# One decode layer on Trainium2: K and V loaded by 512 keys of all heads, weights turned on VectorE, one running sum

## The chip, the cores and the metric

The kernel runs on one core of one Trainium2 chip. The time is that of one execution on the device, in microseconds (us), the median of several runs.

## The reference

One token of two sequences goes through a transformer layer: layer norm, attention over a window of a cache, a residual, layer norm, a gated feed-forward part, a residual. All tensors are bf16.

```python
# x: [2, 1, 640]; k_cache, v_cache: [2, 32, 8192, 192]; wq: [640, 6144]; wo: [6144, 640]
# w_gate, w_up: [640, 1536]; w_down: [1536, 640]
W = min(4096, max(256, 8192 // 4))                     # 2048 keys
q = (layernorm(x) @ wq).reshape(B, 1, 32, 192)          # 32 query heads, 32 K/V heads
k, v = k_cache[:, :, -W:, :], v_cache[:, :, -W:, :]
p = softmax(einsum("bhqd,bhkd->bhqk", q, k) * 192 ** -0.5)
o = einsum("bhqk,bhkd->bhqd", p, v).reshape(B, 1, 6144)
h = x + o @ wo
h2 = h + (gelu(layernorm(h) @ w_gate) * (layernorm(h) @ w_up)) @ w_down
```

With one query per head every byte of K and V is used once: 2 sequences x 32 heads x 2048 keys x 192 x 2 bytes is 50.3 MB for K and the same for V. With the weights the kernel reads 122.3 MB.

## The kernel before

**Groups.** The work is cut into 16 groups `g`. A group is four heads of one sequence with all 2048 keys: partition 4i+h holds 64 consecutive keys (`TPG`) of one head, a run of 24 KB. So K of a group is one transfer of 3 MB, V another (`kv_src`, `load_k`, `load_v`). Four groups make a `J`: the same eight heads of both sequences, which is 1536 rows of wo.

**The ring.** All large transfers go to one SBUF tensor `ring` of 144 KB per partition, cut into six slots of 24 KB: four places for K, two for V, and weights that lie over them at times. `load` puts a transfer in a list in program order; `pump` issues the head of the list once every earlier tenant of its bytes has been told `done`. All of them are issued by SyncE (SP) in that order, so a transfer that waits for its bytes holds back those behind it. The issue stands at L369 of the profile.

**One group on the engines.** `transposes(g, half)` (L579) turns K in pairs of bf16 values seen as float32: three times per half eight TensorE (PE) transposes into one of two PSUM buffers `tpp`, and an eviction to `ktr`, by VectorE (DVE, L593) for the first and third, by ScalarE (ACT, L589) for the second. `scores(g)` (L640) multiplies them with the queries `rq`, masked per head by GpSimd (POOL); DVE adds a mask and takes the maximum (`sm`, `mx`, L649). `softmax(g)` spreads the maximum over the partitions by a small matmul (L656), and ACT takes the exponential (L660) with its row sums `zr`. `e_columns(g)` turns the weights by four matmuls on `sel64` and a masked product on DVE into `ering`. `pv(g)` (L685) multiplies 32 such stationaries with V and accumulates four groups in one PSUM bank `ops`.

**The end of a J.** `z_rows`, `o_rows` and `o_columns` divide by the sum and turn the result into columns `ot` (L699, L709, the DVE product `orow`, L717, L721); `oproj(J)` (L735) multiplies them with its part of wo and adds into `hrow`.

**Order.** Each engine runs its instructions in program order. `_Prog` finds the waits. PE and DVE run the groups in a loop over J, in which e_columns and pv of a group come between the halves of the next group's transposes and behind them:

```python
scores(4 * J)
softmax(4 * J)
for g in range(4 * J + 1, 4 * J + 4):
    transposes(g, 0)
    e_columns(g - 1)
    transposes(g, 1)
    pv(g - 1)
    scores(g)
    softmax(g)
```

K of group 0 is loaded first, then wq, then K of group 1. Behind the loop come `oproj(3)` (L735, L745), the second layer norm (L752 to L813) and the feed-forward part (L824 to L880).

Of the kernel before, what the change touches and what calls it, by code (L numbers as in the profile page):

```python
# [5 lines left out]
BF16 = mybir.dt.bfloat16  # L6
# [6 lines left out]
B = 2  # L13
# [16 lines left out]
WO_BIAS = 32  # L30
RARE = ("oc", "q", "y0")
# [200 lines left out]
SLOT = 24576  # L232
RING = 6 * SLOT
TPG = 64
# [7 lines left out]
WU_AT = K_AT[2]  # L242
WD_AT = (K_AT[2] + 15360, 15360, 19200, 19200 + 2560)


def bass_sequential_preLN__sliding_block_cached__geglu_ffn__decode_kernel(
# [12 lines left out]
    with ExitStack() as ctx:  # L259
# [14 lines left out]
        selw = sb("selw", [128, 2, 128], F32)  # L274
        zsel = sb("zsel", [128, 128], F32)
        mska = sb("mska", [128, 128], F32)
        oh4 = sb("oh4", [128, 4], F32)
        oh16 = sb("oh16", [128, 16], F32)
        mask = sb("mask", [128, 6, 4], F32)
        mask16 = sb("mask16", [128, 16], F32)  # L280
        maskhd = sb("maskhd", [128, 8], F32)
        sel64 = sb("sel64", [128, 64], BF16)
        selq = sb("selq", [128, 32], BF16)
        selb = sb("selb", [128, 2], BF16)
        eps_t = sb("eps_t", [128, 1], F32)
# [27 lines left out]
        rq = sb("rq", [128, 4, 6, 16], BF16)  # L313
        qs = sb("qs", [128, 384], BF16)
        mx = sb("mx", [128, 1], F32)
        mrhs = sb("mrhs", [128, 16], BF16)
        sm = sb("sm", [128, 512], F32)
        gate = sb("gate", [128, 1], F32)
        nm = sb("nm", [128, 1], F32)
        zr = sb("zr", [128, 4], F32)  # L320
        z4 = sb("z4", [128, 4], F32)
        zs = sb("zs", [128, 1], F32)
        rinv = sb("rinv", [128, 1], F32)
        wm = sb("wm", [128, 8], F32)
        eexp = sb("eexp", [128, 512], BF16)
        ering = sb("ering", [128, 4, 32, 32], BF16)
        osb = sb("osb", [128, 384], F32)
        orow = sb("orow", [128, 8, DH], BF16)
        cti = orow[:, :, :].rearrange("p h d -> p (h d)").bitcast(I32)[:, 0:512].rearrange("p (k x) -> p k x", k=4)
        ot = sb("ot", [128, 12, B], BF16)  # L330
# [4 lines left out]
        urow = osb  # L335
# [12 lines left out]
        P.dma_count["wo"] = WO_BIAS  # L348
# [26 lines left out]
        def kv_src(cache, g):  # L375
            h0 = 8 * (g // 4) + 4 * (g % 4 // 2)
            return cache[g % 2, h0:h0 + 4, SKT - WIN:, :].rearrange("h (i t) d -> i h (t d)", t=TPG)

        def load_k(g):
            load(("k", g), K_AT[g % 4], SLOT, kv_src(A_k_cache, g), lambda v: v, f"k{g % 4}")  # L380

        def load_v(g):
            load(("v", g), V_AT[g % 2], SLOT, kv_src(A_v_cache, g), lambda v: v, f"v{g % 4}")
# [5 lines left out]
        def load_wo(J):  # L389
            src = A_wo[1536 * J:1536 * (J + 1), :].rearrange("(p kk) n -> p kk n", kk=12)  # L390
            for i, (k0, k1) in enumerate(wo_parts(J)):
                load(("wo", J, i), WO_AT[J] + 2 * k0 * D, 2 * (k1 - k0) * D, src[:, k0:k1, :],
                     lambda v: v.rearrange("p (kk n) -> p kk n", n=D), "wo" if J < 3 else f"wo{J}{i}")

        def wo_parts(J):
            return ((0, 12),)
# [5 lines left out]
        def load_ffn():  # L402
            load(("wg", 1), K_AT[1], 2 * (NC5 - 1) * F, B_w_gate.rearrange("(p c) f -> p c f", c=NC5)[:, 1:NC5, :],
# [34 lines left out]
        load_k(0)  # L438
        load_wq()
        load_k(1)  # L440
        for g in range(NG):
            if g > 0 and g + 1 < NG:
                load_k(g + 1)
            load_v(g)
            if g % 4 == 3 and g > 3:
                load_wo(g // 4 - 1)
        load_wo(3)
# [3 lines left out]
        BITS = (1, 2, 3, 6, 12, 16, 28, 31, 32, 64, 96)  # L451
# [5 lines left out]
        pool(lambda e: e.memset(ering[:, :, :, :].rearrange("p a b c -> p (a b c)").bitcast(I32), 0), W=[("er", k) for k in range(4)])  # L457
# [12 lines left out]
        dve(tt(pti[:, :], pi[:, :].to_broadcast([128, 11]), bits[:, :], ALU.bitwise_and),  # L470
            R=["pi"] + [("bits", k) for k in range(11)], W=["pti"])
# [40 lines left out]
        for k, pat in enumerate(([[0, 32], [1, 4]], [[0, 16], [2, 4], [0, 2]], [[0, 4], [4, 8], [0, 4]], [[32, 4], [0, 32]])):  # L512
            pool(lambda e, k=k, pat=pat: e.iota(cti[:, k, :], pattern=pat, base=0, channel_multiplier=0), W=[("cti", k)])
        pool(lambda e: e.tensor_copy(cf[:, 1:5, :], cti[:, :, :]), R=[("cti", k) for k in range(4)], W=["cfm"])


        pool(ts(pg[:, 1:2], rb(31), 16.0, ALU.is_lt), R=["pf"], W=["v16"])
        pool(ts(pg[:, 2:3], rb(31), 4.0, ALU.is_lt), R=["pf"], W=["v4"])
        pool(ts(pg[:, 4:5], rb(16), 8.0, ALU.mult, rb(3), ALU.add), R=["pf"], W=["c16"])
        pool(ts(pg[:, 5:6], rb(96), 0.125, ALU.mult, pg[:, 4:5], ALU.add), R=["pf", "c16"], W=["c16b"])  # L520
        pool(ts(pg[:, 6:7], rb(96), 0.5, ALU.mult, rb(1), ALU.add), R=["pf"], W=["c64"])
        pool(ts(pg[:, 7:8], rb(12), 0.5, ALU.mult, pg[:, 6:7], ALU.add), R=["pf", "c64"], W=["c64b"])
        pool(ts(pg[:, 6:7], rb(2), 4.0, ALU.mult, pg[:, 7:8], ALU.add), R=["pf", "c64b"], W=["c64"])
        pool(ts(pg[:, 7:8], rb(16), 64.0, ALU.mult, pg[:, 6:7], ALU.add), R=["pf", "c64"], W=["c64b"])
# [3 lines left out]
        pool(ts(pg[:, 10:11], rb(64), 1.0 / 16.0, ALU.mult, rb(31), ALU.add), R=["pf"], W=["chd"])  # L528
        pool(ts(pg[:, 11:12], rb(3), 2.0, ALU.mult), R=["pf"], W=["p3"])
# [8 lines left out]
        pool(ts(pm[:, :], cf[:, 3, :], rb(28), ALU.is_equal), R=["cfm", "pf"], W=["pm"])  # L538
        pool(ts(oh16[:, :], cf[:, 0, 0:16], pg[:, 5:6], ALU.is_equal), R=["cf0", "c16b"], W=["oh16"])
        pool(ts(sel64[:, :], cf[:, 0, 0:64], pg[:, 7:8], ALU.is_equal), R=["cf0", "c64b"], W=["sel64"])  # L540
        pool(ts(mask16[:, :], cf[:, 2, 0:16], pg[:, 11:12], ALU.is_equal), R=["cfm", "p3"], W=["mask16"])
        pool(ts(mska[:, :], cf[:, 1, :], 4.0, ALU.mult, rb(12), ALU.is_equal), R=["cfm", "pf"], W=["mska"])
        pool(ts(zsel[:, :], mska[:, :], pg[:, 1:2], ALU.mult), R=["mska", "v16"], W=["zsel"])
        pool(ts(mska[:, :], mska[:, :], -1.0, ALU.add, BIG, ALU.mult), R=["mska", "zsel"], W=["mska"])

        def consts_late():
            pool(ts(oh4[:, :], cf[:, 0, 0:4], pg[:, 8:9], ALU.is_equal), R=["cf0", "cq"], W=["oh4"])
            pool(ts(cf[:, 1, :], cf[:, 1, :], 2.0, ALU.mult), R=["cfm", "mska"], W=["cf1"])
            pool(ts(cf[:, 4, :], cf[:, 4, :], 0.25, ALU.mult), R=["cfm"], W=["cf4"])
            pool(tt(cf[:, 1, :], cf[:, 1, :], cf[:, 4, :], ALU.add), R=["cf1", "cf4"], W=["cf1"])  # L550
            pool(ts(cf[:, 3, :], cf[:, 3, :], 1000.0, ALU.mult), R=["cfm", "pm"], W=["cf3"])
# [374 lines left out]
```

## Time and profile before

| | |
|---|---|
| median of three runs | 292.94 us (292.73 to 293.17) |
| profiled execution: time | 292.85 us |
| profiled execution: span of the core | 291.5 us |
| mean granted TensorE clock | 0.874 |
| PE, DVE, ACT, POOL busy | 199.5, 123.8, 76.9, 25.7 us |
| moved by DMA | 122.42 MB at a mean of 420 GB/s |

The page has the busy time of each engine, the span in 40 equal slices (a digit is a share in tenths, GB/s what the DMA engines moved), the chain of waits that ended last, the costliest groups of instructions, and the DMA issues with their size and time to landing. A row of the timeline is: start and length in us, engine, line of the kernel, operation, what is written from what, shapes, count, and in brackets how long the engine had been idle and what ended that. A row of the groups has the busy time of all and the mean length of one in ns.

### The profile page before, as it was taken

How to read it: one execution, taken by the hardware profiler on the slowest of the kernel's cores; microseconds unless marked ns; L12 is line 12 of the kernel's file. 1: busy time of each engine (PE TensorE's matmuls, PEld its weight loads, DVE VectorE, ACT ScalarE, POOL GpSimd, SP SyncE). 2: the span in 40 equal slices, each digit the busy share in tenths (PEclk: the TensorE clock that was granted, in tenths of full speed). 3: DMA queues.
4: the chain of work that ended last, by engine and by line, in shares of the span. 5: the costliest groups of instructions: out<-in, count | busy, mean ns of one | idle time of the engine just before them, and what ended most of it. 6: DMA issues, size and time to landing. Idle time of an engine off the chain costs nothing.

```text
span 291.5 us, 5193 instructions
## 1 busy us (share of the span) xinstructions
PE 199.5 (68%) x2141; PEld 145.3 (50%) x2141; DVE 123.8 (42%) x232; ACT 76.9 (26%) x72; POOL 25.7 (9%) x85
## 2 busy tenths in 40 slices
PE   0670768756866587877776848684957848686885
PEld 0550445636555285654654727362835547563443
DVE  5250035632535444645165525362563525352422
ACT  1050123332232033532320513251313315151001
POOL 8891020000000000000000000000000000000000
PEclk9996699997979779999599998999799969797555
DMA  8999999999999999999999999999999999999994
GB/s 324 432 465 396 430 432 425 427 430 428 428 432 432 432 432 432 432 432 432 416 440 432 432 432 432 429 425 432 424 440 432 428 432 432 432 432 411 426 414 159
DMA packets 6505, 122.42 MB, mean 420 GB/s; under 512 B 734, under 2 KB 864, under 8 KB 1504
## 3 DMA queue, kind: packets, MB, share of 16 engines
q1 hardware_dynamic: 6348, 121.90, 97.7%
q10 hardware_dynamic: 148, 0.40, 0.5%
q8 instruction: 6, 0.10, 0.1%
q14 instruction: 3, 0.02, 0.0%
HBM read 122.29 MB, written 0.00 MB: 419 GB/s over the span
## 4 chain that ended last, share of the span: by engine, by line
DMA 58%; PE 23%; DVE 7%; issue 6%; ACT 4%; SPq 1%; DVEq 0%
DMA ring<-in_A_k_cache_dram 44%; PE tpp L579 12%; DMA ring<-in_A_wq_dram 10%; DMA ring<-in_A_wo_dram 5%; DVE ktr L593 4%; ACT ktr L589 3%; PE ops L685 3%; PE tpp L603 2%; DVE orow L434 1%; PE m L709 1%; PE m L735 1%; SPq L369 1%; DVE ering L434 1%; PE sps L824 1%; PE m L873 1%
## 5 line engine op out<-in xcount | busy, mean ns | idle before, releaser
L579 PE MATMUL tpp<-identf,ring 128*128 128x128 f32 x768 | 113.5, 308 | 38.4 <-DMA ring<-in_A_k_cache_dram 21.0
L579 PEld LDWEIGHTS tpp<-identf,ring 128*128 128x128 f32 x768 | 99.0, 159 | 48.8 <-DMA ring<-in_A_k_cache_dram 22.0
L593 DVE COPY ktr<-tpp 128x2048 bf16<-128x2048 bf16 x64 | 78.4, 1225 | 86.8 <-PE tpp L579 86.4
L589 ACT ACTIVATE ktr<-tpp 128x2048 bf16<-128x2048 bf16 x32 | 60.1, 1877 | 83.6 <-PE tpp L579 83.6
L660 ACT ACTIVATE eexp<-sm,nm 128x512 bf16<-128x512 f32 x16 | 11.5, 722 | 84.3 <-DVE nm L658 84.3
L640 PE MATMUL sps<-ktr,rq 128*16 128x512 bf16 x384 | 25.8, 403 | 1.2 <-POOL rq L434 1.2
L685 PE MATMUL ops<-ring,ering 128*32 128x384 bf16 x512 | 25.0, 340 | 0.0
L649 DVE CUSTOM_DVE_ANT_1 sm<-sps,mska 128x512 f32<-128x512 f32 x16 | 11.0, 686 | 27.9 <-issue 27.9
L434 POOL TENSOR_TENSOR rq<-qs,mask 128x96 bf16<-128x96 bf16 x16 | 5.5, 354 | 170.7 <-PE sps L640 156.7
L685 PEld LDWEIGHTS ops<-ring,ering 128*32 128x32 bf16 x512 | 12.5, 99 | 8.1 <-issue 2.5
L640 PEld LDWEIGHTS sps<-ktr,rq 128*16 128x16 bf16 x384 | 8.7, 89 | 13.9 <-issue 6.6
L656 PE MATMUL m<-mrhs,pm 128*128 128x16 bf16 x16 | 2.9, 184 | 17.2 <-DVE mrhs L430 17.2
L656 PEld LDWEIGHTS m<-mrhs,pm 128*128 128x128 bf16 x16 | 1.5, 96 | 26.0 <-DVE mrhs L430 26.0
L603 PE MATMUL tpp<-ring,xnT 128*32 128x384 bf16 x80 | 5.3, 444 | 9.4 <-DMA ring<-in_A_wq_dram 9.4
L434 DVE TENSOR_TENSOR orow<-m,wm 128x1536 bf16<-128x1536 f32 x4 | 7.0, 1758 | 4.1 <-PE m L709 4.1
L603 PEld LDWEIGHTS tpp<-ring,xnT 128*32 128x32 bf16 x80 | 3.0, 127 | 11.6 <-issue 9.6
L434 DVE TENSOR_TENSOR ering<-m,mask 128x256 bf16<-128x256 f32 x16 | 6.6, 415 | 1.3 <-PE m L669 1.3
L626 DVE CAST qs<-ops 128x384 bf16<-128x384 f32 x1 | 0.6, 557 | 15.0 <-PE ops L621 15.0
L717 PE MATMUL m<-selb,orow 128*128 128x2 bf16 x48 | 3.5, 200 | 4.2 <-DVE orow L434 4.2
L717 PEld LDWEIGHTS m<-selb,orow 128*128 128x128 bf16 x48 | 3.2, 156 | 5.8 <-DVE orow L434 5.8
L709 PE MATMUL m<-osb,selw 128*128 128x192 f32 x16 | 4.4, 405 | 1.9 <-DVE osb L695 1.9
L735 PE MATMUL m<-ring,ot 128*2 128x320 bf16 x96 | 5.5, 381 | 0.0
(124 smaller groups left out, 91.5 us busy)
## 6 DMA issues: line engine op xcount, KB each, us to landing
ring<-in_A_k_cache_dram SPq DMA_DIRECT2D x16, 3072.0 KB, 32.3
ring<-in_A_v_cache_dram SPq DMA_DIRECT2D x16, 3072.0 KB, 26.7
ring<-in_A_wq_dram SPq DMA_DIRECT2D x1, 7680.0 KB, 28.2
ring<-in_A_wo_dram SPq DMA_DIRECT2D x4, 1920.0 KB, 16.3
ring<-in_B_w_gate_dram SPq DMA_DIRECT2D x1, 1536.0 KB, 17.7
ring<-in_B_w_up_dram SPq DMA_DIRECT2D x1, 1536.0 KB, 20.9
ring<-in_B_w_down_dram SPq DMA_DIRECT2D x1, 960.0 KB, 23.3
ring<-in_B_w_down_dram SPq DMA_DIRECT2D x1, 480.0 KB, 24.0
```

Source lines behind the costliest of these rows:

```text
L434: return lambda e: e.tensor_tensor(out=out, in0=a, in1=b, op=op)
L579: ins = e.transpose(tpp[bi][:, 512 * j + 128 * u:512 * j + 128 * (u + 1)], kv[:, off:off + 128], identf[:, :])
L589: act(lambda e, dst=dst, bv=bv: e.activation(out=dst, in_=bv, func=ACT.Copy), W=[("kt", half, k)], X=both)
L593: dve(lambda e, dst=dst, bv=bv: e.tensor_copy(dst, bv.rearrange("p (a x) -> p a x", a=2)), W=[("kt", half, k)], X=both, cls=0)
L603: ins = e.matmul(tps[0][32 * r:32 * (r + 1), 0:384], lhsT=xnT[:, c, 32 * J:32 * (J + 1)], rhs=wq[:, c, 1536 * J + 384 * r:1536 * J + 384 * ...
L640: ins = e.matmul(sps[32 * ch:32 * ch + 16, :], lhsT=rq[:, g % 4, k, :], rhs=ktr[:, k // 2, 1024 * ch + k % 2:1024 * (ch + 1):2], start=(k ...
L649: dve(lambda e: e.tensor_tensor_reduce(out=sm[:, :].rearrange("p (u x) -> p u x", u=4), in0=sps[:, :].rearrange("p (u x) -> p u x", u=4), ...
L660: act(lambda e: e.activation(out=eexp[:, :], in_=sm[:, :], func=ACT.Exp, bias=nm[:, 0:1], scale=1.0, accum_out=zr[:, g % 4:g % 4 + 1]), R= ...
L685: ins = e.matmul(ops_[32 * r:32 * (r + 1), 0:384], lhsT=ering[:, g % 4, t, :], rhs=vv[:, 384 * t:384 * (t + 1)], start=(g % 4 == 0 and t < 4),
L709: pe(lambda e, tp=tp: e.matmul(bank, lhsT=selw[:, tp, :], rhs=osb[:, DH * tp:DH * (tp + 1)], start=(tp == 0), stop=(tp == 1), skip_group_c ...
L717: ins = e.matmul(m2[:, 2 * kk:2 * kk + 2], lhsT=orow[:, :, kk:DH:12], rhs=selb[:, :], start=True, stop=True)
L735: ins = e.matmul(m1[32 * r:32 * r + 2, 192:512], lhsT=ot[:, kk, :], rhs=wo[:, kk - k0, 320 * h:320 * (h + 1)], start=(kk == 1 or J < 3 and ...
```

## The change

- **Loads.** A load is now 512 consecutive keys of all 32 heads of one sequence: partition 4h+r holds 128 keys, a run of 48 KB, 6 MB in all. The ring has three slots of 48 KB: two for K, one for V. A load serves a pair of groups, `2i` and `2i+1`, each with 64 of the 128 keys of every partition. wq is loaded first, before K. All four parts of wo are loaded behind the last V, before the feed-forward weights.
- **Weights.** `e_columns` and its matmuls go; `e_blocks(g)` turns the exponentials by four DVE transposes in blocks of 32x32, one for each quarter of the partitions, into `eblk`.
- **pv.** Each group has 64 matmuls of 192 columns in a bank of its own (`ops` or `m1`), copied to `osb`; pv of both groups of a pair stands behind the second group's softmax and e_blocks.
- **Running sum.** After four groups `weights` and `combine` scale the four results and the sum so far to a common maximum and add them in `osum`. After 8 groups, one sequence, `heads_done(b)` divides and turns the result into columns.
- **wo.** All four `oproj` stand behind the loop, with one accumulation in PSUM.
- **Queries.** `q_rows` stands ahead of the loop, with 64 of its matmuls cut to 192 columns, 112 in all; `rq` is masked in four parts at the start of a sequence.

The core of the diff, with the constants and masks that go with it left out:

```diff
-SLOT = 24576
-RING = 6 * SLOT
-TPG = 64
+SLOT = 49152
+RING = 3 * SLOT
+TPG = 128
+NQ = 4
...
-K_AT = (0, SLOT, 3 * SLOT, 5 * SLOT)
-V_AT = (2 * SLOT, 4 * SLOT)
-WQ_AT = 3 * SLOT + SLOT // 2
-WO_AT = (K_AT[3], K_AT[3], K_AT[3], 0)
+K_AT = (0, SLOT)
+V_AT = 2 * SLOT
+WQ_AT = SLOT
+WO_AT = (0, 15360, 30720, SLOT)
...
-            return cache[g % 2, h0:h0 + 4, SKT - WIN:, :].rearrange("h (i t) d -> i h (t d)", t=TPG)
+        def kv_src(cache, i):
+            t0 = SKT - WIN + NQ * TPG * (i % NQ)
+            return cache[i // NQ, :, t0:t0 + NQ * TPG, :].rearrange("h (r t) d -> h r (t d)", t=TPG)
+
+        def load_k(i):
+            load(("k", i), K_AT[i % 2], SLOT, kv_src(A_k_cache, i), lambda v: v, f"k{i % 2}")
+
+        def load_v(i):
+            load(("v", i), V_AT, SLOT, kv_src(A_v_cache, i), lambda v: v, f"v{i % 2}")
...
-        load_k(0)
         load_wq()
-        load_k(1)
-        for g in range(NG):
...
+        for i in range(2 * NQ):
+            load_k(i)
+            load_v(i)
+        for J in range(4):
+            load_wo(J)
         load_ffn()
...
+        def weights():
+            dve(lambda e: e.tensor_reduce(out=nmin[:, :], in_=nms[:, :], axis=AX.X, op=ALU.min), ...
+            act(lambda e: e.activation(out=wz[:, 0:5], in_=nms[:, :], func=ACT.Exp, bias=nmin[:, 0:1], scale=-1.0), ...
+
+        def e_blocks(g):
+            for hg in range(4):
+                dve(lambda e, hg=hg: e.transpose(eblk[32 * hg:32 * (hg + 1), g % 2, :, hg, :],
+                                                 eexp[32 * hg:32 * (hg + 1), :].rearrange("p (a x) -> p a x", x=32)),
+                    R=["eexp"], W=[("eb", g % 2, hg)], cls=0)
+
+        def pv(g):
+            vv, vtoks = where["v", g // 2]
+            bank, x = ((ops_, "o"), (m1, "m1"))[g % 2]
 
             def fn(e):
...
+                for a in range(16):
+                    for r in range(4):
+                        t = 64 * (g % 2) + 4 * a + r
+                        ins = e.matmul(bank[32 * r:32 * (r + 1), 0:DH],
+                                       lhsT=eblk[:, g % 2, a, :, :].rearrange("p s x -> p (s x)")[:, r:128:4],
+                                       rhs=vv[:, DH * t:DH * (t + 1)], start=(a == 0), stop=(a == 15),
+                                       tile_position=(0, 32 * r), skip_group_check=True)
                 return ins
...
+            if g % 2 == 1:
+                done(("v", g // 2))
+            dve(lambda e: e.tensor_copy(osb[:, g % 4, :], bank[:, 0:DH]), W=[("osb", g % 4)], X=[x], cls=0)
+
+        def combine():
+            dve(lambda e: e.tensor_tensor_reduce(out=z5[:, :], in0=wz[:, 0:5], in1=zr[:, :], ...
+            dve(lambda e: e.tensor_copy(zr[:, 4:5], wz[:, 5:6]), ...
+            dve(lambda e: e.tensor_copy(nms[:, 4:5], nmin[:, :]), ...
+            pe(lambda e: e.matmul(m2[:, 264:270], lhsT=rowsel[:, :], rhs=wz[:, :], start=True, stop=True), ...
+            dve(lambda e: e.tensor_scalar(out=wp[:, :], in0=m2[:, 264:270], scalar1=0.25, scalar2=None, op0=ALU.mult), ...
+            dve(ts(osum[:, :], osum[:, :], wp[:, 4:5], ALU.mult), R=["wp", "osum"], W=["osum"], cls=0)
+            for k in range(4):
+                dve(lambda e, k=k: e.scalar_tensor_tensor(out=osum[:, :], in0=osb[:, k, :], scalar=wp[:, k:k + 1], in1=osum[:, :], ...
+
+        def heads_done(b):
+            dve(lambda e: e.reciprocal(rinv[:, :], wp[:, 5:6]), R=["wp"], W=["rinv"])
+            dve(ts(onrm[:, :], osum[:, :], rinv[:, 0:1], ALU.mult, 0.25, ALU.mult), ...
...
+            for y in range(2):
+                def fn(e, y=y):
+                    for j in range(2):
+                        J = 2 * y + j
+                        ins = e.matmul(sps[:, DH * j:DH * (j + 1)], lhsT=colsel[:, 128 * J:128 * (J + 1)], rhs=onrm[:, :],
+                                       start=True, stop=True, skip_group_check=True)
+                    return ins
+
+                pe(fn, R=["colsel", "onrm"], X=["s"])
+                dve(tt(sm[:, 0:384]..., sps[:, 0:384]..., mask16..., ALU.mult), R=["mask16"], W=["sm"], X=["s"])
+                dve(lambda e: e.tensor_reduce(out=ot32[:, :], in_=sm[:, 0:384]..., axis=AX.X, op=ALU.add), ...
+                dve(lambda e, y=y: e.tensor_copy(ot[:, 2 * y:2 * y + 2, :, b], ot32[:, :]...), R=["ot32"], W=["ot"])
...
+        q_rows()
+        q_stationary()
         looped.append(True)
-        for J in range(5):
...
+        for J in range(4):
+            P.loop_seg("a", J)
+            for g in range(4 * J, 4 * J + 4):
+                transposes(g, 0)
+                if g % 2 == 1:
+                    e_blocks(g - 1)
+                transposes(g, 1)
+                scores(g)
+                softmax(g)
+                if g % 4 == 3:
+                    weights()
+                if g % 2 == 1:
+                    e_blocks(g)
+                    pv(g - 1)
+                    pv(g)
+            combine()
+            if J == 1:
                 P.loop_seg("op", J)
-                oproj(J - 2)
...
+                heads_done(0)
         P.loop_seg()
-        oproj(3)
+        heads_done(1)
+        for J in range(4):
+            oproj(J)
```

More of the change, by code (lines that the diff above doesn't have):

```diff
@@ L29 @@
 BIAS = 16
-WO_BIAS = 32
-RARE = ("oc", "q", "y0")
+RARE = ()
 class _Op:
@@ L389, in load_wo @@
         def load_wo(J):
[L390 to L396, printed above, removed]
+            load(("wo", J), WO_AT[J], 24 * D, A_wo[1536 * J:1536 * (J + 1), :].rearrange("(p kk) n -> p kk n", kk=12),
+                 lambda v: v.rearrange("p (kk n) -> p kk n", n=D), f"wo{J}")
         def load_wg0():
@@ L583, in transposes @@
                 pe(fn, R=ktoks + ["identf"], X=both)
-                if half == 1 and k == 2:
-                    done(("k", g))
+                if g % 2 == 1 and half == 1 and k == 2:
+                    done(("k", g // 2))
                 bv = tpp[bi][:, :].bitcast(BF16)
@@ L706, in o_rows @@
-        def o_rows(J):
-            bank = m2[:, 276:276 + DH]
-            for tp in range(2):
-                pe(lambda e, tp=tp: e.matmul(bank, lhsT=selw[:, tp, :], rhs=osb[:, DH * tp:DH * (tp + 1)], start=(tp == 0),
-                                             stop=(tp == 1), skip_group_check=True), R=[("osb", tp), ("selw", tp)], X=["m2o"])
-            dve(tt(orow[:, :, :], bank.unsqueeze(1).to_broadcast([128, 8, DH]),
-                   wm[:, :].unsqueeze(2).to_broadcast([128, 8, DH]), ALU.mult), R=["wm"], W=["orow"], X=["m2o"])
@@ new lines, in softmax @@
+            dve(lambda e: e.tensor_reduce(out=nms[:, n:n + 1], in_=m2[:, 256:260], axis=AX.X, op=ALU.max, negate=True),
+                W=[("nm", n)], X=["m2"], cls=0)
+            act(lambda e: e.activation(out=eexp[:, :], in_=sm[:, :], func=ACT.Exp, bias=nms[:, n:n + 1], scale=1.0,
+                                       accum_out=zr[:, n:n + 1]), R=[("nm", n), "sm", "gate"], W=["eexp", ("zr", n)])
+        def weights():
+            dve(lambda e: e.tensor_reduce(out=nmin[:, :], in_=nms[:, :], axis=AX.X, op=ALU.min), R=[("nm", k) for k in range(5)],
+                W=["nmin"], cls=0)
+            act(lambda e: e.activation(out=wz[:, 0:5], in_=nms[:, :], func=ACT.Exp, bias=nmin[:, 0:1], scale=-1.0),
+                R=["nmin"] + [("nm", k) for k in range(5)], W=["wz"])
```

312 lines of the change are left out of this document (116 added, 196 removed).

## The prediction

> **What bounds it now.** I read the page from the top: span, slices, the chain that ended last; then the DMA issues, and the queue's own waits (engine, line, releaser: us in total, times, longest).
>
> ```profile
> span 291.5 us, 5193 instructions
> ...
> DMA  8999999999999999999999999999999999999994
> GB/s 324 432 465 396 430 432 425 427 430 428 428 432 432 432 432 432 432 432 432 416 440 432 432 432 432 429 425 432 424 440 432 428 432 432 432 432 411 426 414 159
> ...
> DMA 58%; PE 23%; DVE 7%; issue 6%; ACT 4%; SPq 1%; DVEq 0%
> ...
> ring<-in_A_k_cache_dram SPq DMA_DIRECT2D x16, 3072.0 KB, 32.3
> ...
> ring<-in_A_wq_dram SPq DMA_DIRECT2D x1, 7680.0 KB, 28.2
> ring<-in_A_wo_dram SPq DMA_DIRECT2D x4, 1920.0 KB, 16.3
> ...
> SPq L369 <- PE ops L685: 123.0, 11, 17.1
> ```
>
> The transfers bind: every slice but the ends moves about 432 GB/s. A K or V load (3072 KB, 3.146 MB) takes 7.28 us at that rate; K and V of one group 14.56 us. The queue waits long for V buffers (123 us), but with earlier loads still moving, so the rate never falls. The profiled execution took 292.85 us, span plus 1.35; the median of the runs, 292.94, agrees. What counts is how much shorter than 14.56 us a group's arithmetic is. The timeline of group 1 (start, length, engine, line):
>
> ```profile
> 40.49 1.96 PE L579 MATMUL tpp<-identf,ring 128*128 128x128 f32 x16
> ...
> 42.49 1.88 ACT L589 ACTIVATE ktr<-tpp 128x2048 bf16<-128x2048 bf16 x1 [0.84 <-PE tpp L579]
> ...
> 44.03 1.22 DVE L593 COPY ktr<-tpp 128x2048 bf16<-128x2048 bf16 x1 [1.19 <-PE tpp L579]
> ...
> 45.17 0.41 DVE L434 TENSOR_TENSOR ering<-m,mask 128x256 bf16<-128x256 f32 x1
> 45.55 1.22 DVE L593 COPY ktr<-tpp 128x2048 bf16<-128x2048 bf16 x1
> ...
> 46.83 1.09 PE L579 MATMUL tpp<-identf,ring 128*128 128x128 f32 x8 [0.43 <-DVE ktr L593]
> ...
> 47.85 1.48 PE L685 MATMUL ops<-ring,ering 128*32 128x384 bf16 x32
> 47.96 1.22 DVE L593 COPY ktr<-tpp 128x2048 bf16<-128x2048 bf16 x1 [1.19 <-PE tpp L579]
> ...
> 49.31 1.55 PE L640 MATMUL sps<-ktr,rq 128*16 128x512 bf16 x24
> ...
> 50.93 0.69 DVE L649 CUSTOM_DVE_ANT_1 sm<-sps,mska 128x512 f32<-128x512 f32 x1 [1.74 <-issue]
> ...
> 51.95 0.18 PE L656 MATMUL m<-mrhs,pm 128*128 128x16 bf16 x1 [1.08 <-DVE mrhs L430]
> 52.17 0.17 DVE L658 TENSOR_REDUCE nm<-m 128x1 f32<-128x16 f32 x1 [0.28 <-PE m L656]
> 52.38 0.72 ACT L660 ACTIVATE eexp<-sm,nm 128x512 bf16<-128x512 f32 x1 [4.00 <-DVE nm L658]
> 52.48 1.97 PE L579 MATMUL tpp<-identf,ring 128*128 128x128 f32 x16 [0.35 <-DMA ring<-in_A_k_cache_dram]
> 53.01 0.19 ACT L660 ACTIVATION_READ_ACCUMULATOR eexp<-sm,nm 128x1 f32 x1
> ```
>
> From the first transpose at 40.49 to the end of the maximum's matmul at 52.13 is 11.64 us; only then does PE wait for K. Its exponential (52.38) runs under the next group's transposes, and pv (47.85) fits exactly under the last eviction (47.96 to 49.18), ahead of scores. So 2.9 us of each 14.56 are slack, and nothing of a group's softmax is exposed.
>
> **The pair.** A load is now 6.29 MB, 14.56 us, for two groups; K has two slots, V only one. Per pair the two loads are 29.1 us, with the same bytes as before. Four edits act on the PE order.
>
> (1) In the even group pv is gone from under the last eviction, but scores waits for that eviction anyway: 11.64 us stay. Scores and maximum keep their shapes, the weights' load 32 columns instead of 16; taken at nothing, since it overlaps the streams (a tenth of scores, 0.15 us, if not).
>
> (2) Four DVE transposes of 32 partitions by 512 bf16 replace the four matmuls on sel64 and the 0.41 us product. No row has such a transpose. Rows for its price:
>
> ```profile
> L593 DVE COPY ktr<-tpp 128x2048 bf16<-128x2048 bf16 x64 | 78.4, 1225 | 86.8 <-PE tpp L579 86.4
> ...
> 215.10 0.62 DVE L695 COPY osb<-ops 128x192 f32<-128x192 f32 x2 [0.80 <-PE ops L685]
> ...
> 287.62 1.78 PE L873 MATMUL m<-ring,uT 128*17 128x160 bf16 x48 [0.31 <-DVE uT L434]
> ```
>
> The plain copy moves an element in 0.6 ns (1225 for 2048), so 0.3 us for 512; the product above takes 1.62 ns, so 0.83 us; sm, 512 one at a time, takes 0.69. I take sm's row as nearest, less a little overlap between neighbours (two osb copies need 0.62): 0.62 each, E = 2.5 us a group; bounds 1.2 and 3.3. The Trainium skill (VectorE: DVE Perf Modes, section The three transpose paths) gives 311 ns for a 128x128 bf16 transpose on VectorE; my estimate from that page by plain scaling to 512 elements a row is 1.24 us each, 5 us a group, and the sum below would then be 40 us longer; no row here shows it.
>
> In the odd group E stands on DVE between the evictions of the two halves, where the product pushed the 45.55 eviction by 0.3: the odd group ends its maximum after 11.64 - 0.3 + 2.5 = 13.84 us.
>
> (3) pv of both groups follows in PE order, ahead of the next transposes. pv(g-1) hides under the softmax, pv(g) does not: from the maximum's matmul to exp's release 1.2 us (52.13 to 53.2 and a wake-up), then E again, then pv(g): 0.1 + V. V is 64 matmuls of 192 columns. By columns it is the 1.48 of today's 32 of 384; by count it would be 46 ns each, 2.9 us. The L873 row issues 48 of 160 columns at 37 ns in the slow end of the kernel; I take 30 ns, V = 1.9. So 1.2 + 2.5 + 0.1 + 1.9 = 5.7 us stand bare, with PE idle for about 1.8 of them.
>
> Pair: C = 11.64 + 13.84 + 5.7 = **31.2 us**, against 29.1 of loads.
>
> (4) The one V buffer. V of the next pair is issued when pv(g) of this one is done, some 2 us before data flows (below), and K after next queues behind it on SP. So K after next lands 31.1 us after this pair's end: the queue runs dry whenever C is over 27.1, and at C = 31.2 period and pair length are equal. What is queued behind the new waits: on PE everything, on DVE the next evictions, on SP the next K.
>
> **The boundaries.** Every second pair ends in weights and combine. Rows for these, for the tail and for the start:
>
> ```profile
> 1.44 0.57 SPq L369 DMA_DIRECT2D ring<-in_A_wq_dram  x1
> ...
> 29.82 5.29 PE L603 MATMUL tpp<-ring,xnT 128*32 128x384 bf16 x80 [9.40 <-DMA ring<-in_A_wq_dram]
> ...
> 215.52 0.92 PE L709 MATMUL m<-osb,selw 128*128 128x192 f32 x4 [0.46 <-DVE osb L695]
> ...
> 218.23 0.48 DVE L434 TENSOR_TENSOR hrow<-m,hrow 98x320 f32<-98x320 f32 x1
> ...
> 266.84 0.59 PE L699 MATMUL m<-zr,zsel 128*128 128x4 f32 x2 [0.52 <-DVE ering L434]
> ...
> 275.91 1.77 PE L735 MATMUL m<-ring,ot 128*2 128x320 bf16 x24
> ...
> 277.73 0.49 DVE L745 CUSTOM_DVE_ANT_0 hrow<-m,hrow 98x320 f32<-98x320 f32 x1 [2.46 <-PE m L735]
> ...
> 282.72 0.62 DVE L430 TENSOR_SCALAR sm<-sps,rstd 98x384 f32<-98x384 f32 x1 [1.86 <-PE sps L824]
> ...
> 289.80 0.69 SPq L880 DMA_DIRECT2D out_dram<-yrow  x1
> ```
>
> Combine: osb copy 0.35 and the sum of weights 0.3, the float32 matmul 0.6 as L699, wp 0.2, then osum in five DVE passes over 192 elements, 0.33 each by hrow's 0.48 for 320. PE goes on after 1.4 us, but its first eviction waits behind osum: 2.2 us per boundary, 3.3 to the end of osum; weights' reduce adds 0.2 on the four odd pairs. The old o_rows and o_columns (orow and its matmuls) go, but they stood in DMA slack. heads_done: 0.6 for two small DVE operations, and for each half a float32 matmul pair (0.92) and on DVE 0.6 + 0.6 + 0.2 (sm's size); the second half's matmul overlaps the first's reduce: 4.8 us; in the middle, once, 4.3 of it delay the next eviction.
>
> Start: K0 came first and then wq, landing at 29.8 with 11.01 MB (25.5 us of transfer): 4.2 us are latency and slow first slice. wq and a double K0 are 14.16 MB: K0 lands at 37.0. q_rows, split into 112 matmuls, hides under K0; if it did not, V0 alone would come later. Of these I take 2 us as the time from an issue to its first bytes; were it 4, the last pv would come no later: each K then lands 33.1 us after a pair's end, and the next pair with the boundary before or behind it (2.2) takes 33.4.
>
> Loop: 37.0 + 8 x 31.2 + 3 x 2.2 + 4.3 + 0.8 = 298.3 for the last pv. Tail: osum 3.3, heads_done 4.8, then all of wo: 4 x 1.77 + 0.4 = 7.5 (three of these four stood under loads); from there 277.7 to the span's end at 291.5, 13.8: together 29.4. wo, gate, up, down (13.4 MB, 31 us) follow V7 (issued at about 267 + 2, landed at 283) and end at 314: under the tail. Span 327.7, time **329.0 us**, 36 slower, 12%.
>
> **The rivals.**
>
> *The loads keep binding* (the other side). Place: the wait of V(i+1). It decides at C = 27.1 us; below that, the loads run back to back as now. E of 0.3 (0.07 us a transpose) and V = 1.5 give C = 26.4; with boundaries of 1 us instead of 2.2 the last K lands at 37.0 + 14 x 14.56 = 240.8, the last pv is done at 267.2 and the transfers at 286.4. Today they end about 286.9 (2.7 us of the last slice at 432), 4.6 before the span; so the span is 291, the time 292.3, no change, if the tail runs at full clock (half of 7.1 for wo and 3 us less behind it: 22.9). With the 29.4 it is 298. For it: the slack of 2.9 us a group. Against: two groups' own chains are 23.3 us before any transpose of weights, and E would have to lie under the plain copy's. 4%, half of it not slower.
>
> *All heads at once slows the reads.* 32 heads lie 8192 x 192 x 2 bytes = 3 MiB apart, and the 16 engines now start at such distances; today a load takes four heads and its engines mostly read neighbouring runs. The rows show full rate with four heads, and no wider load. It decides from 403 GB/s down (two loads longer than 31.2 us). At the 324 GB/s of the first slice, a load is 19.4 us, K0 lands at 42, and the loop is 38.8 a pair: 374 + 1.4 = 375 us; at 396, the lowest full slice, 331. The Trainium skill (DMA: Bandwidth & Descriptors, section Latency and other measured facts, on row pitch) speaks against this layout: copies with rows 2 MiB apart ran at 164 GB/s where 512 KiB apart gave 207. By that ratio, an estimate from the page, a load would take 18.4 us. No run here shows it; 3 MiB is no power of two. 9%.
>
> *The clock drops at each pair's end.* A granted clock seen when PE waits:
>
> ```profile
> core 0: us, PE busy (x) PEld busy (x) DVE busy (x) ACT busy (x) POOL busy (x), PEclk, DMA share, GB/s
> 266.00:275.00 9.00, 7.77 (x78) 4.34 (x78) 3.77 (x9) 0.00 (x0) 0.00 (x0) 0.50 1.00 424
> ...
> 67.42 4.51 PE L579 MATMUL tpp<-identf,ring 128*128 128x128 f32 x24 [3.32 <-DMA ring<-in_A_k_cache_dram]
> ```
>
> After 3.3 us idle, 24 transposes take 4.5 us where 3.4 are usual, and two waits of 1.1 us within 2.4 us put the tail at 0.50. The new wait has 1.1 + 1.8 us idle with pv between. If pv(g) and the first transposes run at half clock, a pair is 2 us longer: 345 us. 15%.
>
> **How the numbers follow.** The pair-bound case has 72%; its bounds are E = 1.2 with V = 1.5 (C = 28.25, where the queue's 31.1 shares in the period: 308) and E = 3.3 with V = 2.9 (C = 33.85: 350). The range starts a little under, at 305, for a tail at full clock, and ends at 352, with the clock rival inside and the slow reads left out: 8 in 10. About 0.2% (0.6 us) is what a measurement of this kernel can tell from no change. Faster 0.02, same 0.02, slower 0.96.
>
> **What would show it.** Right: DVE transposes of about 0.6 us, PE idle 1.5 to 2 us just before every second pv, SP's V wait ended by that pv with the DMA engines empty (slices of 7 to 8 tenths in the middle), K landed before PE asks, and some 29 us from the last pv to the end, the last 13 without a transfer. Wrong: slices of 9 throughout at a lower GB/s (reads), slices of 9 at 432 (loads still bind), a clock of 0.5 at pair ends, or transposes far from 0.6 us.

## The result and the profile after

The changed kernel takes **355.68 us**, the median of six runs (348.51 to 359.93), against 292.84 us (292.55 to 293.32): ratio 1.191, 95% interval 1.188 to 1.194. Two of the six runs took 348.5 and 349.3 us at a granted clock of 0.88 to 0.89 and four took 354 to 360 us at 0.79 to 0.84, and the ratios in this document go by runs of the first kind. The forecast was 329.0 us in a range of 305 to 352: by the ratio the time is 349 us, inside it near its upper end, while the median of all six lies 4 us above it. The profiled execution took 349.29 us, 20.3 more than the forecast's sum.

The page of the changed kernel, from the top: span, clock by slices, the DMA engines by slices, the chain that ended last; then groups (line, engine, operation, tiles, count | busy us, mean ns | idle before, what ended it), DMA issues, and the queue's own wait.

```profile
span 347.7 us, 6049 instructions
...
PEclk9999978569959998999697998997899888988579
DMA  9999999629995999499959980799699949999950
GB/s 351 453 418 424 381 435 401 263 92 452 449 424 212 424 407 441 164 430 401 452 226 407 452 363 0 311 413 452 271 362 452 447 187 362 410 426 434 415 218 2
...
PE 29%; DVE 28%; issue 25%; DMA 11%; ACT 5%; DVEq 1%; SPq 0%; ACTq 0%
...
L555 PE MATMUL tpp<-identf,ring 128*128 128x128 f32 x768 | 105.4, 292 | 45.4 <-DVE ktr L569 34.9
...
L651 DVE STREAM_TRANSPOSE eblk<-eexp 32x512 bf16<-32x512 bf16 x64 | 44.9, 701 | 7.8 <-ACT eexp L640 6.3
L620 PE MATMUL sps<-ktr,rq 128*32 128x512 bf16 x384 | 35.4, 517 | 22.3 <-DVE ktr L569 22.3
...
ring<-in_A_k_cache_dram SPq DMA_DIRECT2D x8, 6144.0 KB, 31.6
ring<-in_A_v_cache_dram SPq DMA_DIRECT2D x8, 6144.0 KB, 17.5
...
SPq L370 <- PE m L663: 252.5, 8, 40.5
```

DMA was 58% of the chain and is now 11%; the DMA row has a hole in the middle once a pair, as the forecast asked for, and the queue's eight waits all end with pv on the m bank, the second of a pair. Between the holes the engines move up to 453 GB/s, so the long runs are not read more slowly. The mean granted clock, 0.882, is no lower than before (0.874); but a fall now lengthens the chain, where before there was slack. One pair, from its first transpose to the issue of the next V (start, length, engine, line; in brackets the engine's idle time and what ended it):

```profile
143.28 1.96 PE L555 MATMUL tpp<-identf,ring 128*128 128x128 f32 x16
...
152.11 1.54 PE L620 MATMUL sps<-ktr,rq 128*32 128x512 bf16 x24 [1.39 <-DVE ktr L569]
...
154.85 0.18 PE L636 MATMUL m<-mrhs,pm 128*128 128x4 bf16 x1 [1.20 <-DVE mrhs L426]
154.89 1.95 PE L555 MATMUL tpp<-identf,ring 128*128 128x128 f32 x16
...
157.27 1.09 PE L555 MATMUL tpp<-identf,ring 128*128 128x128 f32 x8 [0.44 <-DVE ktr L569]
...
159.54 2.89 DVE L651 STREAM_TRANSPOSE eblk<-eexp 32x512 bf16<-32x512 bf16 x4
...
163.75 1.97 PE L555 MATMUL tpp<-identf,ring 128*128 128x128 f32 x8 [2.97 <-DVE ktr L569]
...
167.11 2.75 PE L620 MATMUL sps<-ktr,rq 128*32 128x512 bf16 x24 [1.39 <-DVE ktr L569]
...
171.06 0.18 PE L636 MATMUL m<-mrhs,pm 128*128 128x4 bf16 x1 [1.19 <-DVE mrhs L426]
171.16 1.52 PE L663 MATMUL ops<-ring,eblk 128*32 128x192 bf16 x64
...
172.32 2.90 DVE L651 STREAM_TRANSPOSE eblk<-eexp 32x512 bf16<-32x512 bf16 x4 [0.69 <-ACT eexp L640]
...
175.28 1.52 PE L663 MATMUL m<-ring,eblk 128*32 128x192 bf16 x64 [2.59 <-DVE eblk L651]
...
176.84 0.53 SPq L370 DMA_DIRECT2D ring<-in_A_v_cache_dram  x1
```

The even group takes 11.75 us (143.28 to 155.03, where the maximum's matmul ends), as forecast. In the odd group the weights' transposes on DVE (159.54) stand ahead of an eviction, TensorE waits 2.97 us for it, and what follows runs at half speed: eight transposes in 1.97 us where eight took 1.09 at 157.27, scores in 2.75 where the even group's took 1.54; the granted clock from 163.7 to 171.2 us is 0.54. The bare end, with its second set of transposes and two pv of 1.52 us, runs at full speed.

The windows from one pair's end to the next (busy us of each engine with counts, then the granted clock, the DMA share and GB/s):

```profile
38.50:74.90 36.40, 25.18 (x275) 18.94 (x276) 17.92 (x27) 9.14 (x8) 0.92 (x2) 0.72 0.75 325
74.90:108.50 33.60, 21.87 (x274) 16.23 (x274) 18.54 (x29) 9.33 (x9) 1.93 (x4) 0.85 0.89 376
108.50:143.40 34.90, 20.16 (x277) 14.86 (x278) 20.73 (x39) 9.14 (x8) 0.00 (x0) 0.95 0.85 361
143.40:176.80 33.40, 20.47 (x274) 14.98 (x274) 18.50 (x29) 9.34 (x9) 1.94 (x4) 0.90 0.89 377
176.80:218.50 41.70, 24.70 (x285) 18.71 (x286) 24.36 (x47) 9.14 (x8) 0.00 (x0) 0.88 0.71 302
320.40:347.70 27.30, 16.59 (x262) 10.15 (x254) 10.36 (x37) 1.27 (x4) 0.00 (x0) 0.75 0.54 221
```

Numbered from 0, pair 0 takes 36.4 us, an ordinary one (1, 3 and 5; 3 is the one shown) 33.5, one that begins with combine (2 and 6) 34.9, and pair 4, with combine and heads_done, 41.7. The last pv ends at 321.0; the tail from there is 26.7.

### The profile page after: what moved, and what is told of

Its sections match the earlier page's. It is cut to its first block, busy times and chain, and to the rows that moved or that the text cites. A ratio compares the mean times of both kernels' runs of the same rounds, so it can differ in the third digit from the quotient of the medians.

```text
span 347.7 us, 6049 instructions
## 1 busy us (share of the span) xinstructions
PE 197.5 (57%) x2573; PEld 145.1 (42%) x2573; DVE 173.1 (50%) x323; ACT 77.7 (22%) x76; POOL 22.0 (6%) x67
## 2 busy tenths in 40 slices
DMA packets 4202, 122.44 MB, mean 352 GB/s; under 512 B 478, under 2 KB 608, under 8 KB 1248
## 4 chain that ended last, share of the span: by engine, by line
PE 29%; DVE 28%; issue 25%; DMA 11%; ACT 5%; DVEq 1%; SPq 0%; ACTq 0%
PE tpp L555 19%; DMA ring<-in_A_k_cache_dram 11%; DVE eblk L651 11%; DVE ktr L569 9%; PE m L663 4%; ACT ktr L565 3%; DVE sm L628 2%; ACT eexp L640 2%; PE sps L697 2%; DVE osum L686 2%; PE m L720 1%; DVE mrhs L426 1%; PE m L636 1%; PE m L680 1%; DVE sm L430 0%
## 5 line engine op out<-in xcount | busy, mean ns | idle before, releaser
L555 PE MATMUL tpp<-identf,ring 128*128 128x128 f32 x768 | 105.4, 292 | 45.4 <-DVE ktr L569 34.9
L555 PEld LDWEIGHTS tpp<-identf,ring 128*128 128x128 f32 x768 | 90.1, 149 | 57.9 <-DVE ktr L569 42.6
L651 DVE STREAM_TRANSPOSE eblk<-eexp 32x512 bf16<-32x512 bf16 x64 | 44.9, 701 | 7.8 <-ACT eexp L640 6.3
L620 PE MATMUL sps<-ktr,rq 128*32 128x512 bf16 x384 | 35.4, 517 | 22.3 <-DVE ktr L569 22.3
L640 ACT ACTIVATE eexp<-sm,nms 128x512 bf16<-128x512 f32 x16 | 11.6, 723 | 97.9 <-DVE nms L638 97.9
L620 PEld LDWEIGHTS sps<-ktr,rq 128*32 128x32 bf16 x384 | 11.4, 114 | 38.9 <-issue 22.8
L663 PE MATMUL m<-ring,eblk 128*32 128x192 bf16 x512 | 13.5, 263 | 18.3 <-DVE eblk L651 18.3
L663 PEld LDWEIGHTS m<-ring,eblk 128*32 128x32 bf16 x512 | 11.4, 113 | 20.4 <-DVE eblk L651 20.3
L663 PE MATMUL ops<-ring,eblk 128*32 128x192 bf16 x512 | 14.6, 277 | 0.0
L663 PEld LDWEIGHTS ops<-ring,eblk 128*32 128x32 bf16 x512 | 12.5, 117 | 0.2
```

Of the source, the lines that this page charges most:

```text
L555: ins = e.transpose(tpp[bi][:, 512 * j + 128 * u:512 * j + 128 * (u + 1)], kv[:, off:off + 128], identf[:, :])
L620: ins = e.matmul(sps[32 * hg:32 * (hg + 1), :], lhsT=rq[:, k, hg, :], rhs=cols, start=(k == 0), stop=(k == 5), tile_position=(0, 32 * hg))
L640: act(lambda e: e.activation(out=eexp[:, :], in_=sm[:, :], func=ACT.Exp, bias=nms[:, n:n + 1], scale=1.0, accum_out=zr[:, n:n + 1]), R=[(" ...
L651: dve(lambda e, hg=hg: e.transpose(eblk[32 * hg:32 * (hg + 1), g % 2, :, hg, :], eexp[32 * hg:32 * (hg + 1), :].rearrange("p (a x) -> p a ...
L663: ins = e.matmul(bank[32 * r:32 * (r + 1), 0:DH], lhsT=eblk[:, g % 2, a, :, :].rearrange("p s x -> p (s x)")[:, r:128:4], rhs=vv[:, DH * t ...
```

## The experiments

The theory after this reading: the pair is a chain of arithmetic, as forecast, with the clock's fall after the 2.97 us wait on top; the loads behind the one V buffer bind nothing at 33.5 us a pair. The rivals: the clock is not the cause, the loads are, or the weights' transposes cost more than their own time.

**e1_warm: keep TensorE busy in the long wait.** 44 matmuls of the identity with itself, results unused, ahead of the last transposes of an odd group:

```diff
+                if g % 2 == 1 and half == 1 and k == 2:
+                    warm(44)
```

> Adds 44 matmuls of 128 columns (identity by identity, result unused) on TensorE in the wait of 2.97 us that each pair's odd group has before its last eight transposes. Theory (the wait lets the granted clock fall, and so lengthens what follows it): the last transposes return from 1.97 to 1.09 us and the odd scores from 2.75 to 1.55, 1.2 to 2.1 us a pair, 8 pairs: 333 to 340 us, although work was added. Rival (the odd scores are slow for another reason, such as their new way through K or VectorE's traffic): odd scores stay at 2.75 and the time at 348 to 351.

It took 336.25 us (333.94 to 339.15), ratio 1.147 (1.140 to 1.154). Its timeline, the same place, and two pair ends:

```profile
153.85 2.62 PE L545 MATMUL m<-identb 128*128 128x128 bf16 x44
156.99 1.09 PE L563 MATMUL tpp<-identf,ring 128*128 128x128 f32 x8 [0.52 <-DVE ktr L579]
159.48 1.56 PE L630 MATMUL sps<-ktr,rq 128*32 128x512 bf16 x24 [1.39 <-DVE ktr L579]
...
71.58 0.54 SPq L370 DMA_DIRECT2D ring<-in_A_v_cache_dram  x1
...
102.95 0.54 SPq L370 DMA_DIRECT2D ring<-in_A_v_cache_dram  x1
```

The eviction comes no sooner, but the eight transposes are back at 1.09 and scores at 1.56. The ordinary pair is 31.4 us (71.58 to 102.95) where it was 33.5, one with combine 33.7 where it was 34.9, and the span 333.3 where it was 347.7. Work added made the kernel 14 us faster: the clock is shown to be the cause of that much.

**e2_late: take the wait away instead.** The even group's weights are transposed after all evictions of the odd group:

```diff
                 transposes(g, 0)
+                transposes(g, 1)
                 if g % 2 == 1:
                     e_blocks(g - 1)
-                transposes(g, 1)
```

> Only the place of e_blocks(g-1) on VectorE changes: behind the evictions of the second half instead of between the halves. Theory (the engines' chain of a pair sets the time, with E between the evictions on it): the 2.97 us wait goes, the maximum of the odd group waits about 1.2 us for the transposes instead, and the clock stays up, 3.2 us a pair: 323 us (318 to 333 without part of the clock's share). Rival (loads behind the one V buffer set the period): no change, over 340.

332.65 us (331.69 to 337.85), ratio 1.134 (1.131 to 1.136): above the 323 expected, at the upper end of what was allowed for, and below the rival's 340. Its timeline:

```profile
155.42 1.60 PE L620 MATMUL sps<-ktr,rq 128*32 128x512 bf16 x24 [1.39 <-DVE ktr L569]
159.28 0.18 PE L636 MATMUL m<-mrhs,pm 128*128 128x4 bf16 x1 [2.26 <-DVE mrhs L426]
159.39 2.29 PE L663 MATMUL ops<-ring,eblk 128*32 128x192 bf16 x64
163.50 2.75 PE L663 MATMUL m<-ring,eblk 128*32 128x192 bf16 x64 [1.83 <-DVE eblk L651]
```

The 2.97 us are gone and scores is fast, but the transposes now hold up the maximum (2.26 us of wait where 1.19 was), and after that wait the two pv of this pair take 2.29 and 2.75 us where 1.52 is full speed.

**e8b_late_warm: both.** e2_late with 34 idle matmuls ahead of the maximum's and 38 between the two pv:

```diff
+                if g % 2 == 1:
+                    warm(34)
...
                     pv(g - 1)
+                    warm(38)
                     pv(g)
```

> This is e2_late with idle identity matmuls added on TensorE where it would stand still: 34 ahead of the maximum's matmul of the odd groups and 38 between the two pv sums; their results are used by nothing. Theory (the lower granted clock after a wait is what e2_late still paid: its pv took 2.29 and 2.75 us in place of 1.5): the two pv sums go back to some 1.5 us each, about 1 to 2 us less per pair over 8 pairs, so 318 to 326 us against e2_late's 332.65. Rival (the clock is not what it paid, the order alone is): 331 to 338, the idle work at best hidden.

329.75 us (329.03 to 331.61), ratio 1.127 (1.123 to 1.131): 2.9 us below e2_late, not the 7 to 15 of the theory, and just below the rival's 331; the intervals of the two ratios touch, so the gain is hardly clear of the noise. The group of the pv on the m bank, first in e2_late, then here:

```profile
L663 PE MATMUL m<-ring,eblk 128*32 128x192 bf16 x512 | 16.0, 292 | 15.9 <-DVE eblk L651 15.9
```

```profile
L671 PE MATMUL m<-ring,eblk 128*32 128x192 bf16 x512 | 12.2, 248 | 2.6 <-DVE eblk L659 2.6
```

All matmuls of pv are at full speed now, which is worth 16.0 - 12.2 = 3.8 us on the m bank. I had taken 1.2 us a pair from one pair of the timeline; the row of the group says that only some of the eight were slow. (The other pv is hidden under the softmax, at either speed.) That the spans differ by about as much (331.9 and 328.2) is in part chance. Pair 1 took 33.7 us here and 30.0 in e2_late, since TensorE stopped within its first pv for 2.04 us, for which the trace shows no cause:

```profile
98.44 0.36 PE L671 MATMUL ops<-ring,eblk 128*32 128x192 bf16 x6 [2.04 <-issue]
```

All the rest of the span is 7.4 us shorter than in e2_late, near the lower end of the theory. Whether the other executions had that stop isn't known, so this run doesn't decide how much the clock still cost there.

**e3_halfv: half the bytes of V.** Only the first half of each V run is loaded, and both groups of a pair multiply with it:

```diff
-            load(("v", i), V_AT, SLOT, kv_src(A_v_cache, i), ...
+            load(("v", i), V_AT, SLOT // 2, kv_src(A_v_cache, i)[:, :, 0:64 * DH], ...
```

> Loads only the first half of every V run (24 of 48 KB) and multiplies both groups of a pair with it, so half of V is left out. Theory (engines bind in the loop, K lands before TensorE asks): 347 to 350 us, no change, though 25.2 MB less are read. Rival (loads, or V's wait for its one buffer, bind): a pair loses up to 7.3 us of transfer, 300 to 330 us.

353.62 us (351.64 to 355.69), ratio 1.206 (1.199 to 1.213): 25.2 MB less (97.27 for 122.44) and not faster. From the second issue of V to the seventh the changed kernel takes 177.01 us, this one 177.12:

```profile
74.94 0.54 SPq L370 DMA_DIRECT2D ring<-in_A_v_cache_dram  x1
...
251.95 0.54 SPq L370 DMA_DIRECT2D ring<-in_A_v_cache_dram  x1
```

```profile
76.08 0.54 SPq L370 DMA_DIRECT2D ring<-in_A_v_cache_dram  x1
...
253.20 0.53 SPq L370 DMA_DIRECT2D ring<-in_A_v_cache_dram  x1
```

So neither the one V buffer nor the bytes bind the loop. The few us more lie at the ends; the mean granted clock of the span is 0.844 for 0.882, and why it is lower is open.

**e4_oneblock: one of four transposes.** Only the first of the four 32-partition blocks of the weights is turned:

```diff
-            for hg in range(4):
+            for hg in range(1):
```

> One VectorE transpose per group instead of four (three quarters of the weights are left out; their blocks stay zero). Theory: E falls from 2.9 to 0.72, twice on the chain of a pair, and the clock's 2 us go with the wait: C is 27.1 to 29 instead of 33.5. Then the loads behind V's one buffer begin to bind (the period cannot fall under 29.1 and holes appear from 27.1 up): 306 to 314 us. Engines alone would give 297. Rival (transposes are covered): 345 or more.

315.07 us (309.25 to 318.71), ratio 1.062 (1.055 to 1.070): the median just above the 306 to 314 expected, the ratio (311 us) inside. By the ratios (1.191 and 1.062), six transposes less a pair are worth some 38 us, where 48 of them by their own 0.70 us are 34. A new wait, of four times and 12.0 us, shows what is next:

```profile
L555 PE MATMUL tpp<-identf,ring 128*128 128x128 f32 x768 | 105.7, 293 | 33.5 <-DVE ktr L569 13.5 <-DMA ring<-in_A_k_cache_dram 12.0 <-ACT ktr L565 7.9
```

**e5_one_half: e4 with half of V.** The edit of e3 on e4.

> Both together: one VectorE transpose per group (three quarters of the weights left out) and half of every V run loaded (half of V left out). Theory (with E nearly gone, loads behind the one V buffer bind): now the shorter V loads gain what they didn't gain alone: 297 to 304 us, 9 to 12 below the kernel with one transpose and whole loads, and no wait for K. Rival (after E something else on the engines binds): no lower than that kernel's 309 to 318.

302.02 us (297.76 to 304.91); the wait for K is 1.5 us where it was 12.0. The same half of V that gained nothing in e3_halfv gains some 12 to 13 us here: with three quarters of the transposes gone, the loads bind in part, by the holes in the profile of e4_oneblock those behind the one V buffer.

**e6_onev: one V buffer in the kernel before.** Nothing else is changed:

```diff
-V_AT = (2 * SLOT, 4 * SLOT)
+V_AT = (2 * SLOT, 2 * SLOT)
```

> The kernel before with one V slot of 24 KB instead of two, nothing else. Theory: pv stands 8 us into the next group there, K of the group after next is queued behind it, and a load is issued every 14.6 us before the last one has ended, so the queue stays fed: 292.5 to 295 us. Rival (the single V buffer by itself is what costs): a hole of 2 us or more per group, 16 groups, 310 us or more.

305.56 us (301.98 to 310.52), ratio 1.037 (1.030 to 1.045): neither case. I had reckoned 2 us of latency and 7.3 of transfer for V, 9.3; measured was 12.9 from issue to landing:

```profile
ring<-in_A_v_cache_dram SPq DMA_DIRECT2D x16, 3072.0 KB, 12.9
...
PE tpp L579 <- DMA ring<-in_A_k_cache_dram: 23.7, 11, 3.8
...
PE ops L685 <- DMA ring<-in_A_v_cache_dram: 8.4, 3, 5.1
...
124.98 1.64 PE L685 MATMUL ops<-ring,ering 128*32 128x384 bf16 x32 [2.84 <-DMA ring<-in_A_v_cache_dram]
126.40 2.78 PE L640 MATMUL sps<-ktr,rq 128*16 128x512 bf16 x24
```

TensorE waits 8.4 us for V, where the kernel before never did, and 23.7 for K where it waited 21.0. By my reckoning, 12.9 and a pv of 1.5 are 14.4 of the 14.56 us that a group has, which leaves no slack. And after the 2.84 us for V, scores is at half speed (2.78 for 1.53) in this kernel too.

**e7_pipe: the same work in another order.** Loads, layout, transposes, pv and running sum are those of the change. The loop is written out; a group's transposes of weights are spread between the next group's evictions; pv of a pair comes after the scores of the next even group; the next K is queued ahead of V, and two parts of wo ahead of the last V:

```diff
+            transposes(g, 0, {2: (0,)})
+            transposes(g, 1, {0: (1,), 2: (2, 3)})
             scores(g)
+            if g > 0 and g % 2 == 0:
...
+                pv(g - 2)
+                pv(g - 1)
             softmax(g)
```

> The changed kernel with the same loads, transposes, pv and running sum in another order: four transposes spread between the evictions of the next group, pv of both groups behind the scores of the group after, combine there too, K of the next pair queued ahead of V, two parts of wo ahead of the last V; the loop written out. Theory (it is the order that costs, not the layout or the transposes as such): the bare 5.6 us and the 2.97 us wait go, a pair takes 26.5 to 28 us, the loads of 29.1 bind in the loop, and the longer start and tail remain: 296 to 304 us. Rival (layout, 48 KB runs or the transposes cost by themselves): 320 or more.

302.53 us (301.42 to 304.87), ratio 1.036 (1.030 to 1.041). The page of e7_pipe, its span and the DMA engines by slices:

```profile
span 300.4 us, 5707 instructions
...
DMA  8999999999999999999999999999999999999970
```

The row is full again, with the same 48 KB runs and the same 64 transposes on DVE. Some 47 us of the change's 56 are the order of the work and of its loads (349.3 of the profiled execution against 301.7), not its parts. Several moves were made at once, so their shares aren't told apart.

**e9_pipe2: its two ends.** The last V goes into the even K's slot, free earlier, and the first K comes in two halves with wq between:

```diff
+            load(("v", i), V_AT if i < 7 else 0, SLOT, ...
...
+        for h in range(2):
+            load(("k", 0, h), SLOT // 2 * h, SLOT // 2, ...
+            if h == 0:
+                load_wq()
```

> This is e7_pipe with two edits at its ends: the last V goes into the slot of the even K, free earlier than the V slot, with the output weights' last quarter behind it and the first three in the V slot; and the first K is loaded in two halves with the query weights between them, so that its transposes begin ahead of q_rows. Theory (what e7_pipe's 302.5 holds over 292.8 is the late last V, landed at 270.4, and the late start): the last V lands some 10 us earlier, the last pv ends at 266 to 270, and the time is 291 to 298. Rival (the ends of the loop are set by the transposes and the order on PE, not by these loads): 300 or more.

300.07 us (297.00 to 300.74), ratio 1.025 (1.023 to 1.027): 2 us better, and on the rival's side of 300. The end of its loop and the first matmul of heads_done:

```profile
265.52 2.76 PE L671 MATMUL ops<-ring,eblk 128*32 128x192 bf16 x64
268.06 2.02 PE L671 MATMUL m<-ring,eblk 128*32 128x192 bf16 x64
...
273.10 1.65 PE L707 MATMUL sps<-onrm,colsel 128*128 128x192 f32 x4 [3.01 <-DVE nms L702]
```

The last pv ends at 270.1, at the edge of what the theory said, and waits for no load; but 25.6 us follow it, as in e7_pipe (274.8 to 300.4), all arithmetic: running sum, heads_done, and the wo products, now behind it all. No version here beats the kernel before: the bytes are the same, and its loads were already back to back.

## Why the prediction was right, and where its sum was short

Direction and mechanism held: the pair's own arithmetic took the place of the transfers, and the 349 us of the ratio lie in the range, near its upper end. The point is 20 us short of the profiled execution. Term by term, spans of 327.7 and 347.7 us; the first three lines are parts of a pair, those below them add up:

| term | forecast | measured | on the sum |
|---|---|---|---|
| even group | 11.64 | 11.75 (pair 3) | |
| odd group, to the maximum's end | 13.84 | 16.35 (pair 3), 15.5 (pairs 2, 4, 6, 7) | |
| bare end | 5.7 | 5.56 (pair 3) | |
| K0 lands | 37.0 | 38.5 | +1.5 |
| pair 0 | 31.2 | 36.4 | +5.2 |
| pairs 1, 3, 5, with the weights' reduce | 31.4 | 33.5 | +2.1 x 3 |
| pairs 2, 6, with combine | 33.4 | 34.9 | +1.5 x 2 |
| pair 4, with combine and heads_done | 37.7 | 41.65 | +3.95 |
| pair 7 | 31.4 | 34.15 | +2.75 |
| tail | 29.4 | 26.7 | -2.7 |

The last seven lines add up to the 20.0. (By the prediction's own terms its bounds of C are 28.2 and 33.8, not 28.25 and 33.85, which is half a microsecond of the time.)

*E, the transposes.* Each took 0.70 us, not 0.62, 2.9 with their ends for E = 2.5: the row chosen as nearest (sm, 0.69) was right, the discount for overlap was not. The estimate of 1.24 us by plain scaling of the figure in the Trainium skill (VectorE: DVE Perf Modes, The three transpose paths) is ruled out by the 701 ns row.

*The odd group is the step that failed.* It was costed as 11.64 - 0.3 + E, at full clock. E gave 0.4 of the error. The clock gave 2.1 in pairs 1, 3 and 5, 0.9 in the last transposes and 1.2 in scores. In pairs 2, 4, 6 and 7 it gave 1.2, in scores alone: the eight transposes behind the same wait were still at full speed there. These are the amounts that e1_warm gives back.

```profile
131.18 1.09 PE L555 MATMUL tpp<-identf,ring 128*128 128x128 f32 x8 [2.97 <-DVE ktr L569]
```

The sum said that E stands between the evictions; it didn't say that TensorE stands still meanwhile, and so didn't ask what that does to the clock. The profile of before had rows that could have told: behind waits for K shorter than the 3.32 us that the prediction quotes, 24 transposes were as slow.

```profile
174.12 4.38 PE L579 MATMUL tpp<-identf,ring 128*128 128x128 f32 x24 [2.60 <-DMA ring<-in_A_k_cache_dram]
```

*The clock rival acted, in another place.* It put 2 us a pair on pv(g) and the next transposes, behind the waits of 1.1 and 1.8 us at the pair's end. There pv takes 1.52 us and the transposes (143.28) 1.96 in the pair shown, at full speed: 2.59 us of wait with pv before it did no harm. Only behind pair 6 were the next transposes slow (24 in 4.4 us), which is the better part of what pair 7 took more. Elsewhere the fall comes behind 2.97 us in the odd group. That its 345 us for the whole is 4 from what was measured is luck. The forecast without it is what e1_warm shows: its ordinary pair is 31.4 us against C = 31.2.

*V* was 1.52 us for 64 matmuls, 24 ns each, and not 1.9: the columns price it, not the count. That covered for E in the bare end.

*Boundaries and ends.* Combine cost 2.3 us, as forecast: the even group behind it took 14.0 us (108.5 to 122.5) where 11.7 is usual; the pair is only 1.4 longer than an ordinary one because its odd group kept the fast transposes. heads_done cost 41.7 - 34.9 = 6.8 us, not 4.3: its float32 matmuls took 1.6 us a half where the row of before had 0.92, and the next transposes were slow as well. Pair 0 was at a clock of 0.72. The tail was shorter, its four wo products in 4.9 us where 7.5 were reckoned from a row at half clock.

*The one V buffer* does what the forecast said, between bounds only: no price at C = 33.5 (e3_halfv), a price when the chain is shorter (e4_oneblock against e5_one_half, whose ordinary pairs are 27 to 30 us). Whether 27.1 is the point isn't settled by these: in e4_oneblock short pairs and pairs that wait for K take turns.

*Loads keep binding* is dead by the holes in the DMA row. *Slow reads* are dead by e7_pipe's full row, and by single slices of 452 and 453 GB/s with heads 3 MiB apart. The rule on row pitch that was weighed there (the Trainium skill, DMA: Bandwidth & Descriptors, Latency and other measured facts) is one of powers of two, and this pitch is none.

## What to carry to other kernels

When transfers no longer hide the arithmetic, write out one period of each engine's order and mark where the matmul engine stands still: a wait of 3 us in the midst of steady work cost its own length and 1 to 2 us more. Before costing such an effect for every period, read the group's row over the whole run, not one period's timeline. And a change whose parts look dear may owe its loss to their order: the same loads and the same transposes ran 47 us apart.

## What was not expected of the hardware

- Matmuls of no use made the kernel faster: 44 of them in a wait of 2.97 us brought the mean granted clock from 0.88 to 0.95 and the time from 349.3 to 334.9 (profiled executions). The Trainium skill (TensorE: Matmul & The Clock Gate, What's actually happening) puts the fall to half speed at an idle window of about 3.4 us; here it came behind waits of 2.97 us, and of 2.84 in e6_onev, though not always at once: in four pairs of the changed kernel, and in e6_onev, the first matmuls behind the wait were still fast, and those after them slow. In e2_late it came behind 2.26 us in some pairs and not in others (pv of 2.29 us in the pair shown).
- With one V buffer, a 3 MB load landed after 12.9 us, not the 9.3 of latency and transfer. For the V of 112.15 us (e6_onev) the engines were nearly idle when it was issued (49 GB/s in the microsecond from 112), but K was issued 0.6 us behind it, and from 113 to 125 us the engines moved 4.6 MB, so V's 3.1 MB did not have them to itself.
- A DVE transpose of 32 partitions by 512 bf16 takes 0.70 us; 64 matmuls of 192 columns on 32-wide tiles take 1.52 us at full clock.
